# Complex-gate tree per head pair replaced by a real-decay tree over eight heads per chunk, with phases moved onto q and k

## Chip, cores and metric

One core of a Trainium2 chip runs the program. The metric is device time in microseconds (us) from the first to the last instruction of that core. Runs of the kernel before: 1729.12, 1729.69 and 1709.76 us, median 1729.12.

## What is computed

Four batches, eight heads, 768 tokens, head size 48; then a two-matrix block over 3072 tokens. Inputs are float32, the two weight matrices float64, the result float32.

```python
scale = np.minimum(mag, 0.999) / (mag + 1e-06)      # mag = |a_re + i a_im|
a = (a_re + 1j * a_im) * scale
for t in range(S):                                  # S is a 48 x 48 complex state per head
    S = a[:, :, t, :, None] * S + k[:, :, t, :, None] * v[:, :, t, None, :]
    y[:, :, t] = einsum('bhd,bhde->bhe', q[:, :, t], S.real)
x = y as (3072, 384)
h = x @ w_in                                        # 384 x 2048
out = (maximum(h, 0) + alpha * minimum(h, 0)) @ w_out   # 2048 x 384
```

## The kernel before, in words

A *unit* (`unit`, L182) is two heads of one batch over all 768 tokens: head 0 on partitions 0 to 47, head 1 on 64 to 111. There are 16 units, run two at a time. Each loads q, k, a_re, a_im and v (`load`, L87), makes the gates on VectorE (L193 to L209, with two RECIPROCALs), and climbs a binary tree of seven levels (h = 1, 2, ..., 64 tokens, L231 to L287). On a level TensorE multiplies k and q for all six 128-token chunks (L239, one matmul for the real part and one for the imaginary part, each with K = 48 rows and 128 weight columns), VectorE multiplies K, Q and T by complex products of the other half's gates (L256 to L279, four operations for each complex product, with two cross terms), and a predicated copy (L283) puts the level's products into the attention matrix A. Then the state passes from chunk to chunk (L289 to L314) and the result y comes from A times v and Q times the state (L317 to L331).

The second part (`mlp`, L335) takes one batch in two groups of 384 tokens: transposes of x (L343), 16 blocks of hidden features (three matmuls each, L352; two ScalarE activations L356 and L357; one VectorE operation L358), then three output blocks of 16 matmuls (L365), a copy (L368) and a store from GpSimd's queue (L370). The float64 weights are turned into float32 by `to_f32` (L111) in 40 pieces of one DMA, two ScalarE, four VectorE and two GpSimd operations each.

The order is written out by hand at L373 to L397: after every step of a unit one step of the second part of the *batch before* is issued (in the first batch a step of the weights). The second part of the last batch runs alone at the end. All loads go through SP's queue, in program order. Every float32 matmul appears as two records in the trace.

Of the kernel before, what the change touches and what calls it, by code (L numbers as in the profile page):

```python
# [9 lines left out]
U8 = mybir.dt.uint8  # L10
# [3 lines left out]
PSUM = bass.MemoryType.PSUM  # L14

# [3 lines left out]
SQ_FLOOR = 2.0 ** -116  # lower end of the square root's range  # L19
# A float64's high word, read as a float32: that of 2**-126, where float32's normal numbers begin.  # L20
# [4 lines left out]
def kernel(  # L25
    ctx: ExitStack,
    tc: tile.TileContext,
    q: bass.AP,      # (B, H/2, 2, D, S)
    k: bass.AP,      # (B, H/2, 2, D, S)
    v: bass.AP,      # (B, H/2, 128, S/128, 2*D)  # L30
    a_re: bass.AP,   # (B, H/2, 2, D, S)
    a_im: bass.AP,   # (B, H/2, 2, D, S)
    w_in: bass.AP,   # (H*D, DF)
    w_out: bass.AP,  # (DF, H*D)
    alpha: bass.AP,  # (128, DF/128)
    out: bass.AP,    # (B*S, H*D)
):
# [12 lines left out]

    A unit is two heads of one batch: head 0 on partitions 0.., head 1 on partitions 64.. .
    """
    nc = tc.nc
    B, HP, _, D, S = q.shape
    DM, DF = w_in.shape
    NCH = S // P            # chunks of a batch
    NK = DM // P
    NF = DF // P
    W = 64 + D              # partitions of a unit
    HC = P // 2             # tokens of a chunk that lie in second halves  # L60
    GC = NCH // 2           # chunks of one group of tokens in the second part
    GT = GC * P
    LEVELS = [1 << i for i in range(7)]

    consts = ctx.enter_context(tc.tile_pool(name="consts", bufs=1))
    ld = ctx.enter_context(tc.tile_pool(name="ld", bufs=1))
    work = ctx.enter_context(tc.tile_pool(name="work", bufs=2))
    ps2 = ctx.enter_context(tc.tile_pool(name="ps2", bufs=2, space=PSUM))
    ps1 = ctx.enter_context(tc.tile_pool(name="ps1", bufs=2, space=PSUM))

    def rows(i):
        return slice(64 * i, 64 * i + D)

# [1 line left out]
    q_buf = [ld.tile([W, S], F32, tag=f"q{i}", name=f"q{i}") for i in range(2)]  # L75
    a_buf = [ld.tile([W, 2, S], F32, tag=f"a{i}", name=f"a{i}") for i in range(2)]
    k_buf = [ld.tile([W, 2, S], F32, tag=f"k{i}", name=f"k{i}") for i in range(4)]
    for t in q_buf:
        nc.gpsimd.memset(t[32:64], 0.0)
    for t in a_buf:  # L80
        nc.vector.memset(t[32:64], 0.0)
    for t in k_buf:
        nc.gpsimd.memset(t[32:64, 0], 0.0)

    loaded = {}

    def load(u):  # L87
        b, hp = divmod(u, HP)
        qt, at, kt = q_buf[u % 2], a_buf[u % 2], k_buf[u % 4]
        vt = work.tile([P, NCH, 2 * D], F32, tag="v", name="v", bufs=4)  # L90
        for i in range(2):
            nc.sync.dma_start(at[rows(i), 0], a_re[b, hp, i])
            nc.sync.dma_start(at[rows(i), 1], a_im[b, hp, i])
        for i in range(2):
            nc.sync.dma_start(qt[rows(i)], q[b, hp, i])
            nc.sync.dma_start(kt[rows(i), 0], k[b, hp, i])
        nc.sync.dma_start(vt, v[b, hp])
        loaded[u] = (qt, at, kt, vt)

    load(0)  # L100
    load(1)
# [20 lines left out]
        # numbers below float32's normal ones become 0  # L122
# [4 lines left out]
        # sign, exponent and the first 20 bits of the mantissa  # L127
# [5 lines left out]
        # the other 32 bits, by the power of two  # L133
# [8 lines left out]
    def weights():  # L142
        if w_in.dtype == F32:
# [4 lines left out]
        for c in range(NK):  # L148
            for f in range(0, DF, 256):
# [8 lines left out]
    ident = consts.tile([P, P], F32, tag="ident")  # L158
    make_identity(nc, ident)
    masks = {}  # L160
    for h in LEVELS:
        nb = HC // h
        m = work.tile([P, nb, h], F32, tag="mask", name="mask")
        nc.gpsimd.memset(m, 1.0)
        nc.gpsimd.affine_select(out=m, in_=m, pattern=[[-2 * h, nb], [0, h]], base=0,
                                channel_multiplier=1, compare_op=ALU.is_ge, fill=0.0)
        nc.gpsimd.affine_select(out=m, in_=m, pattern=[[2 * h, nb], [0, h]], base=h - 1,
                                channel_multiplier=-1, compare_op=ALU.is_ge, fill=0.0)
        masks[h] = consts.tile([P, NCH, HC], U8, tag=f"mask{h}", name=f"mask{h}")
        nc.vector.tensor_copy(masks[h], m.rearrange("p n h -> p (n h)").unsqueeze(1)  # L170
                              .to_broadcast([P, NCH, HC]))

# [1 line left out]
    x_of = {}  # L174

    def halves(t, h):
        """A (re, im) or plain row of tokens as (..., block, half, token)."""
        if len(t.shape) == 3:
            return t.rearrange("p r (n s h) -> p r n s h", s=2, h=h)
        return t.rearrange("p (n s h) -> p n s h", s=2, h=h)  # L180

    def unit(u):  # L182
        b, hp = divmod(u, HP)
        qt, at, kt, vt = loaded.pop(u)
        Q = work.tile([W, 2, S], F32, tag="Q", name="Q")
# [13 lines left out]
        nc.scalar.activation(mag, sq, AF.Sqrt)  # L199
        # one Newton step brings the table's root to float32: twice the magnitude  # L200
        nc.vector.reciprocal(rec, mag)  # L201
        nc.vector.tensor_tensor(out=rec, in0=rec, in1=sq, op=ALU.mult)
        nc.vector.tensor_tensor(out=mag, in0=mag, in1=rec, op=ALU.add)
        nc.vector.tensor_scalar(out=rec, in0=mag, scalar1=0.5, scalar2=MAG_EPS, op0=ALU.mult, op1=ALU.add)
# [26 lines left out]
        for h in LEVELS:  # L231
# [16 lines left out]
            def over(t):  # L248
                return t.unsqueeze(2).to_broadcast(sh)
# [125 lines left out]
    for u in range(0, B * HP, 2):  # L375
        b = u // HP
        if u % HP == 0 and b:
            for _ in dense:
                pass
# [14 lines left out]
    for _ in dense:  # L394
        pass
# [40 lines left out]
```

## Time and profile before

| what | value |
|---|---|
| median of 3 runs | 1729.12 us |
| span of the profiled execution | 1729.1 us |
| mean granted TensorE clock | 0.834 of 2.4 GHz |
| TensorE busy | 1421.9 us |
| VectorE busy | 1326.3 us |
| ScalarE busy | 244.1 us |
| GpSimd busy | 169.0 us |
| moved by DMA | 42.28 MB, 18034 packets |

The span is the whole device time; nothing lies around it. "Busy" of TensorE counts any time with a matmul in flight, so it overstates useful work. DVE is VectorE, ACT ScalarE, POOL GpSimd, SP the queue of loads; PEld are TensorE's weight loads.

### The profile page before, as it was taken

Reading aid. Unit: us, or ns where it says so; the run is one execution under the profiler, and the core shown is the slowest. Engines: PE = TensorE matmul, PEld = TensorE weight load, DVE = VectorE, ACT = ScalarE, POOL = GpSimd, SP = SyncE. Lnnn points to the kernel's source line nnn. Section 1 sums busy time; section 2 is a strip of 40 time slices with the busy share of each in tenths; the row PEclk is TensorE's granted clock in tenths of the full one; section 3 lists DMA queues with packets and bytes.
Section 4 is the critical chain, followed back from the end, with each engine's and each line's share of the span. In section 5 each row is a group of like instructions: output and inputs, shape, how many; then the busy total and the mean of one; then the engine's idle time right before and its main releaser. Section 6 shows DMA issues by size and latency. Waiting matters only on the chain.

```text
span 1729.1 us, 21531 instructions
## 1 busy us (share of the span) xinstructions
PE 1421.9 (82%) x8808; PEld 1078.1 (62%) x8808; DVE 1326.3 (77%) x2298; ACT 244.1 (14%) x498; POOL 169.0 (10%) x153
## 2 busy tenths in 40 slices
PE   1456924558889998899889998899889998899998
PEld 1455824557656685678566775678566775678555
DVE  7999689995699829993799849982899749981210
ACT  2000111101201121001211120001201120001321
POOL 3222335551000000000000000000000000000000
PEclk9999999999979959775779868765779868665999
DMA  5211113100010001000010001000010000000000
GB/s 120 66 32 31 46 46 87 46 28 21 7 42 1 17 26 27 16 15 21 14 35 1 29 14 41 1 15 25 10 35 1 15 1 0 5 10 1 1 14 14
DMA packets 18034, 42.28 MB, mean 24 GB/s; under 512 B 3472, under 2 KB 3472, under 8 KB 17936
## 3 DMA queue, kind: packets, MB, share of 16 engines
q1 hardware_dynamic: 16400, 36.20, 8.0%
q0 software_dynamic: 1536, 4.72, 0.7%
q8 instruction: 69, 1.13, 0.3%
q14 instruction: 29, 0.24, 0.0%
HBM read 36.18 MB, written 4.72 MB: 24 GB/s over the span
## 4 chain that ended last, share of the span: by engine, by line
DVE 43%; issue 35%; PE 19%; ACT 1%; POOL 1%; DMA 0%; POOLq 0%; DVEq 0%; SPq 0%; ACTq 0%
PE ps_y L325 6%; DVE A L283 5%; PE ps_y L321 4%; DVE Q L268 4%; DVE rec L205 3%; DVE k L261 3%; DVE kx L260 3%; PE ps_o L365 3%; PE ps_lvl L239 2%; DVE rec L201 2%; DVE Q L270 2%; DVE tx L274 2%; PE ps_h L352 2%; DVE qx L267 2%; DVE Q L269 2%
## 5 line engine op out<-in xcount | busy, mean ns | idle before, releaser
L239 PE MATMUL ps_lvl<-Q,k 48*128 48x64 f32 x4992 | 426.3, 340 | 175.3 <-DVE A L283 160.2
L239 PEld LDWEIGHTS ps_lvl<-Q,k 48*128 48x128 f32 x4992 | 409.5, 249 | 231.4 <-issue 228.4
L352 PE MATMUL ps_h<-xT,w_in_sb 128*128 128x384 f32 x768 | 322.6, 576 | 0.0
L365 PE MATMUL ps_o<-w_out_sb,g 128*128 128x384 f32 x768 | 299.5, 535 | 21.7 <-DVE g L358 21.7
L352 PEld LDWEIGHTS ps_h<-xT,w_in_sb 128*128 128x128 f32 x768 | 168.9, 227 | 117.2 <-issue 44.1
L365 PEld LDWEIGHTS ps_o<-w_out_sb,g 128*128 128x128 f32 x768 | 153.9, 207 | 127.0 <-DVE g L358 24.7
L358 DVE SCALAR_TENSOR_TENSOR g<-neg,nal,g 128x384 f32<-128x384 f32 x128 | 81.1, 633 | 168.8 <-ACT neg L357 168.8
L325 PE MATMUL ps_y<-St,Q 48*128 48x48 f32 x640 | 167.2, 412 | 0.0
L283 DVE COPY_PREDICATED A<-mask,ps_lvl 128x384 f32<-128x384 uint8 x224 | 158.1, 720 | 0.0
L325 PEld LDWEIGHTS ps_y<-St,Q 48*128 48x128 f32 x640 | 141.5, 313 | 19.8 <-issue 5.8
L370 POOL DMA_DIRECT2D out_dram<-ot x24 | 13.1, 548 | 1237.6 <-ACT ot L368 1237.6
L218 PE MATMUL ps_diag<-q,k 48*128 48x128 f32 x384 | 55.7, 370 | 91.8 <-DVE A L221 83.3
L321 PE MATMUL ps_y<-v,A 128*128 128x48 f32 x384 | 115.7, 417 | 0.0
L356 ACT ACTIVATE g<-ps_h 128x384 f32<-128x384 f32 x128 | 62.9, 491 | 372.6 <-PE ps_h L352 367.0
L218 PEld LDWEIGHTS ps_diag<-q,k 48*128 48x128 f32 x384 | 47.7, 259 | 103.8 <-issue 58.8
L201 DVE RECIPROCAL rec<-mag 112x768 f32<-112x768 f32 x16 | 79.2, 4951 | 38.4 <-ACT mag L199 38.4
L261 DVE TENSOR_TENSOR k<-k,T 112x768 f32<-112x768 f32 x96 | 94.7, 987 | 11.8 <-PE ps_lvl L239 11.6
L321 PEld LDWEIGHTS ps_y<-v,A 128*128 128x128 f32 x384 | 91.5, 306 | 14.5
L267 DVE TENSOR_TENSOR qx<-Q,T 112x768 f32<-112x768 f32 x96 | 100.5, 1047 | 0.0
L139 POOL TENSOR_TENSOR rest<-rest,power 128x256 f32<-128x256 f32 (+1 forms) x40 | 74.3, 1857 | 233.6 <-DVE power L135 217.0
L268 DVE TENSOR_TENSOR Q<-Q,T 112x768 f32<-112x768 f32 x96 | 95.8, 998 | 0.0
L260 DVE TENSOR_TENSOR kx<-k,T 112x768 f32<-112x768 f32 x96 | 94.1, 981 | 0.0
(68 smaller groups left out, 1295.7 us busy)
## 6 DMA issues: line engine op xcount, KB each, us to landing
raw<-in_w_in_dram SPq DMA_DIRECT2D x24, 256.0 KB, 2.8
raw<-in_w_out_dram SPq DMA_DIRECT2D x16, 384.0 KB, 3.1
a<-in_a_re_dram SPq DMA_DIRECT2D x32, 144.0 KB, 3.3
a<-in_a_im_dram SPq DMA_DIRECT2D x32, 144.0 KB, 3.6
q<-in_q_dram SPq DMA_DIRECT2D x32, 144.0 KB, 2.8
k<-in_k_dram SPq DMA_DIRECT2D x32, 144.0 KB, 2.9
v<-in_v_dram SPq DMA_DIRECT2D x16, 288.0 KB, 2.8
out_dram<-ot POOLq DMA_DIRECT2D x24, 192.0 KB, 2.1
```

The lines of the kernel that those rows point to most:

```text
L201: nc.vector.reciprocal(rec, mag)
L218: nc.tensor.matmul(ps[:, i, c * P:(c + 1) * P], lhsT=kt[rows(i), 0, cols], rhs=qt[rows(i), cols], start=True, stop=True)
L239: nc.tensor.matmul(ps[:, i, c * HC:(c + 1) * HC], lhsT=kt[rows(i), r, cols], rhs=halves(Q[rows(i), r, cols], h)[:, :, 1], start=(r == 0), ...
L260: nc.vector.tensor_tensor(out=cross, in0=kf, in1=over2(second[:, 1]), op=ALU.mult)
L261: nc.vector.tensor_tensor(out=kf, in0=kf, in1=over2(second[:, 0]), op=ALU.mult)
L267: nc.vector.tensor_tensor(out=cross, in0=qs, in1=over2(first[:, 1]), op=ALU.mult)
L268: nc.vector.tensor_tensor(out=qs, in0=qs, in1=over2(first[:, 0]), op=ALU.mult)
L283: nc.vector.copy_predicated(halves(A[:, i].rearrange("p c t -> p (c t)"), h)[:, :, 1], masks[h].rearrange("p c (n h) -> p (c n) h", h=h), ...
L321: nc.tensor.matmul(y, lhsT=A[:, i, c], rhs=vt[:, c, i * D:(i + 1) * D], start=True, stop=(c == 0))
L325: nc.tensor.matmul(y, lhsT=Q[rows(i), r, c * P:(c + 1) * P], rhs=St[rows(i), c - 1, r], start=False, stop=(r == 1))
L352: nc.tensor.matmul(ps, lhsT=w_in_sb[:, kk, f * P:(f + 1) * P], rhs=xT[g][:, kk], start=(kk == 0), stop=(kk == NK - 1))
L365: nc.tensor.matmul(ps, lhsT=G[f][:, c * P:(c + 1) * P], rhs=w_out_sb[:, f], start=(f == 0), stop=(f == NF - 1))
```

## The change

The first part is rewritten.

- *Gates.* Now made for groups of 384 tokens (eight groups, `gates(g)`), with all 384 rows (8 heads x 48) on 128 partitions x 3. The magnitude goes to a DRAM scratch as a real decay. The unit phases are multiplied up over the tokens (a scan in blocks of 8, then 8 x 8, then 6, with a carry between the groups of a batch), and cos and sin go to the same DRAM scratch. Ten multiplications of a group are on VectorE for group 0 and on GpSimd for the others.
- *Unit.* Now one 128-token chunk of one batch with all eight heads (24 units). q and k are loaded twice, on partitions 0 to 47 and 48 to 95, and one VectorE operation multiplies them by cos and sin. After that one matmul with K = 96 stands for the real part, and decays are real: one VectorE operation per level for Q and K together; the products T of decays are made by GpSimd.
- *Array tiles.* A level's matmuls take 64 weight columns and 64 moving columns, for two heads in the two column halves. y is made transposed, from 64-row halves of v and the level's products, in 64 x 64 tiles; v's halves are loaded separately for each level (levels 2 to 32 through a DRAM copy, `first_halves`).
- *Second part.* y goes to DRAM and comes back as xT, with no transposes. The activation is one ScalarE and one VectorE operation (max(h,0) + alpha min(h,0) = h + (1 - alpha) max(-h,0)). The output store moves to SP.
- *Order.* Units start every 6 slots and take 11 steps, so two are alive; gates of the next group, v's copies and the second part of the group before are spread evenly over the slots (18 slots to a group).

The core of the diff (new lines; loads and most of the gates left out):

```python
def gates(g):
    mul = nc.vector if g == 0 else nc.gpsimd
    ab = work.tile([P, 2, NK, GT], F32, tag="ab", bufs=1)      # GT = 384 tokens, NK = 3
...
    nc.scalar.activation(d, c, AF.Abs_reciprocal_sqrt)
    nc.scalar.activation(e, d, AF.Square)
    mul.tensor_tensor(out=e, in0=e, in1=c, op=ALU.mult)
    nc.vector.scalar_tensor_tensor(out=d, in0=e, scalar=3.0, in1=d, op0=ALU.subtract, op1=ALU.mult)
    mul.tensor_tensor(out=c, in0=c, in1=d, op=ALU.mult)
    yield
...
    for j in range(1, L):                                      # L = 8, nb = 144
        nc.vector.tensor_tensor(out=mm, ...)                   # 4 * nb elements
        nc.vector.tensor_tensor(out=uv[:, 0, :, j], in0=mm[:, 0, 0], in1=mm[:, 1, 1], op=ALU.subtract)
        nc.vector.tensor_tensor(out=uv[:, 1, :, j], in0=mm[:, 0, 1], in1=mm[:, 1, 0], op=ALU.add)
...
def first_halves(b):                                           # 20 DMAs, DRAM to DRAM, runs of 96 elements
    for i, h in enumerate(LEVELS[1:-1]):
        for n in range(HP):
            nc.sync.dma_start(dst.rearrange("c (m h) e -> m h c e", h=h), src)
            yield
...
def load(u):                                                   # 16 DMAs on SP for one unit
    for i in range(2):
        rows = slice(i * D, (i + 1) * D)
        nc.sync.dma_start(KQ[rows, 0], qv[b, :, :, cols])      # rows of 128 tokens: 512 bytes
        nc.sync.dma_start(KQ[rows, 1], kv_in[b, :, :, cols])
    for i in range(2):
        rows = slice(i * D, (i + 1) * D)
        nc.sync.dma_start(PP[rows], scr[i, :, :, cg * P:(cg + 1) * P])
        nc.sync.dma_start(T[rows], scr[2, :, :, cg * P:(cg + 1) * P])
...
def unit(u, loaded):
    nc.vector.tensor_tensor(out=KQ, in0=KQ, in1=PP.unsqueeze(1).to_broadcast([D2, 2, H, P]), op=ALU.mult)
    yield
    def meet(name, weights, moving, n):
        t = ps.tile([P, HP, n], F32, tag="lv", bufs=2)
        for p in range(4):
            for i in range(2):
                nc.tensor.matmul(t[64 * i:64 * i + 64, p], lhsT=weights(4 * i + p),
                                 rhs=moving(KQ[:, 0, 4 * i + p]), start=True, stop=True)
        if name == HC:
            nc.scalar.copy(A[name], t)
        else:
            nc.vector.tensor_tensor(out=A[name], in0=t, in1=masks[name]..., op=ALU.mult)
...
    for h in LEVELS[1:]:                                       # Ts[2]: 512 elements, then 256, ... 8
        nc.gpsimd.tensor_tensor(out=Ts[2 * h], in0=t[:, :, 0], in1=t[:, :, 1], op=ALU.mult)
    yield
...
    for h in LEVELS[1:]:
        meet(h, first(h), second(h), HC)                       # first(h): a ScalarE copy into W
        nc.vector.tensor_tensor(out=both, in0=both, in1=Ts[h]..., op=ALU.mult)   # 1024 elements
        yield
...                                                            # 8 transposes, 8 matmuls: the state
    nc.gpsimd.tensor_tensor(out=St, in0=before, in1=Ts[P]..., op=ALU.mult)
    nc.vector.tensor_tensor(out=St, in0=St, in1=t, op=ALU.add)
    yield
    for s in range(2):
        for name in [1, "odd"] + LEVELS[1:]:
            for e in range(2):
                for i in range(2):
                    nc.tensor.matmul(o, lhsT=Vp[name][64 * i:64 * i + 64, s, e * D:(e + 1) * D],
                                     rhs=A[name][64 * i:64 * i + 64, 2 * s + e], ...)
...                                                            # 8 matmuls with the state before; y to DRAM
def mlp(g):
    nc.sync.dma_start(xT, ysc_of.pop(g).rearrange("(k p) s -> p k s", p=P))
    yield
...
    nc.scalar.activation(neg, t, AF.Relu, scale=-1.0)
    nc.vector.scalar_tensor_tensor(out=gt, in0=neg, scalar=rest_al[:, f:f + 1], in1=t,
                                   op0=ALU.mult, op1=ALU.add)
...
for _ in gates(0): pass
for _ in first_halves(0): pass
while live or slot <= NU * LAG + LAG or beside:                # LAG = 6, PER = 18 slots
    g, at = divmod(slot, PER)
    if at == 0 and g + 1 < NG:
        beside.append(spread(gates(g + 1), slot, slot + PER - LAG, 15))
    if at == LAG and 0 < g <= NG:
        beside.append(spread(mlp(g - 1), slot, slot + PER, 29))
    u, at = divmod(slot, LAG)
    if at == 0 and u < NU:
        live[u] = unit(u, loads.pop(u))
    for n in sorted(live): ...                                 # one step of each live unit
    if at == LAG - 1 and u + 1 < NU:
        loads[u + 1] = load(u + 1)
    ...                                                        # then the steps of beside that are due
```

## Rows read from the trace of the kernel before

**Rows 1.** The page's busy times, then its chain that ended last

```profile
PE 1421.9 (82%) x8808; PEld 1078.1 (62%) x8808; DVE 1326.3 (77%) x2298; ACT 244.1 (14%) x498; POOL 169.0 (10%) x153
...
DVE 43%; issue 35%; PE 19%; ACT 1%; POOL 1%; DMA 0%; POOLq 0%; DVEq 0%; SPq 0%; ACTq 0%
```

**Rows 2.** Windows: us, busy per engine (instructions), granted clock, DMA share, GB/s

```profile
129.70:172.90 43.20, 26.00 (x234) 25.21 (x234) 43.20 (x88) 3.20 (x9) 11.05 (x10) 1.00 0.10 31
...
475.50:518.70 43.20, 35.67 (x232) 25.49 (x232) 43.20 (x61) 4.31 (x9) 0.00 (x0) 0.74 0.18 42
907.80:951.00 43.20, 40.52 (x341) 29.45 (x340) 43.20 (x90) 5.78 (x12) 0.00 (x0) 0.92 0.01 1
1556.20:1599.40 43.20, 41.16 (x190) 35.14 (x189) 7.87 (x36) 4.69 (x12) 0.00 (x0) 0.50 0.00 0
1599.40:1729.10 129.70, 124.89 (x387) 73.21 (x386) 19.81 (x32) 31.66 (x72) 3.23 (x6) 0.99 0.02 10
```

**Rows 3.** TensorE's timeline: start us, length us, line, records, idle before

```profile
905.90 2.94 PE L239 MATMUL ps_lvl<-Q,k 48*128 48x64 f32 x48
...
1545.04 5.41 PE L239 MATMUL ps_lvl<-Q,k 48*128 48x64 f32 x48 [1.22 <-DVE A L283]
1552.76 2.37 PE L304 MATMUL ps_kv<-v,KT 128*64 128x48 f32 x40
1574.07 1.09 PE L321 MATMUL ps_y<-v,A 128*128 128x48 f32 x4
1575.09 1.09 PE L325 MATMUL ps_y<-St,Q 48*128 48x48 f32 x4
...
1600.93 30.48 PE L352 MATMUL ps_h<-xT,w_in_sb 128*128 128x384 f32 x94
```

**Rows 4.** VectorE's groups by line and shape: busy us, mean ns of one

```profile
L358 DVE SCALAR_TENSOR_TENSOR g<-neg,nal,g 128x384 f32<-128x384 f32 x128 | 81.1, 633 | 168.8 <-ACT neg L357 168.8
L201 DVE RECIPROCAL rec<-mag 112x768 f32<-112x768 f32 x16 | 79.2, 4951 | 38.4 <-ACT mag L199 38.4
L270 DVE TENSOR_TENSOR Q<-Q,qx 112x384 f32<-112x384 f32 x112 | 65.7, 587 | 0.0
L208 DVE TENSOR_TENSOR a<-a,rec 112x1536 f32<-112x1536 f32 x16 | 28.6, 1786 | 0.0
L203 DVE TENSOR_TENSOR mag<-mag,rec 112x768 f32<-112x768 f32 x16 | 15.3, 954 | 0.0
L125 DVE SCALAR_TENSOR_TENSOR top<-top,raw 128x256 f32<-128x256 f32 x24 | 10.5, 438 | 12.0 <-ACT top L124 12.0
L129 DVE TENSOR_SCALAR num<-top 128x256 uint32<-128x256 uint32 x24 | 6.8, 284 | 0.0
L279 DVE TENSOR_TENSOR T<-T,tx 112x12 f32<-112x12 f32 x16 | 3.2, 199 | 0.0
```

**Rows 5.** GpSimd beside VectorE: timeline, start us, length us

```profile
189.83 0.72 POOL L139 TENSOR_TENSOR rest<-rest,power 128x256 f32<-128x256 f32 x1 [2.58 <-DVE power L135]
...
254.43 0.99 POOL L139 TENSOR_TENSOR rest<-rest,power 128x384 f32<-128x384 f32 x1 [3.30 <-DVE power L135]
...
341.74 8.24 POOL L140 TENSOR_TENSOR w_out_sb<-num,rest 128x384 f32<-128x384 f32 x1
...
349.04 1.03 DVE L283 COPY_PREDICATED A<-mask,ps_lvl 128x384 f32<-128x384 uint8 x2
...
355.11 1.75 DVE L268 TENSOR_TENSOR Q<-Q,T 112x768 f32<-112x768 f32 x1
```

**Rows 6.** ScalarE's groups by line and shape

```profile
L193 ACT ACTIVATE Q<-a 112x1536 f32<-112x1536 f32 x16 | 23.9, 1494 | 2.7 <-DMA a<-in_a_im_dram 2.7
L193 ACT ACT_TABLE_LOAD x1 | 1.3, 1283 | 6.4 <-DMA a<-in_a_im_dram 6.4
```

**Rows 7.** DMA: the load queue's packets; a load; one issue on SP

```profile
q1 hardware_dynamic: 16400, 36.20, 8.0%
...
k<-in_k_dram SPq DMA_DIRECT2D x32, 144.0 KB, 2.9
...
4.77 0.42 SPq L96 DMA_DIRECT2D k<-in_k_dram  x1
```

More of the change, by code (lines that the diff above doesn't have):

```diff
@@ L71, in rows @@
[L71 to L90, printed above, removed]
-        for i in range(2):
[L92 to L98, printed above, removed]
@@ L100, with halves, mask @@
-    load(0)
-    load(1)
+    dram = ctx.enter_context(tc.tile_pool(name="dram", bufs=2, space=DRAM))
+    ps = ctx.enter_context(tc.tile_pool(name="ps", bufs=1, space=PSUM))
+    def halves(t, h):
+        return t.rearrange("p (n s h) -> p n s h", s=2, h=h)
+    ident = consts.tile([P, P], F32, tag="ident")
+    make_identity(nc, ident)
+    masks = {}
+    def mask(name, h, s):
+        m = work.tile([P, P // h, h * s], F32, tag="mask", name="mask", bufs=1)
+        nc.gpsimd.memset(m, 1.0)
+        nc.gpsimd.affine_select(out=m, in_=m, pattern=[[-h, P // h], [0, h * s]], base=0,
+                                channel_multiplier=1, compare_op=ALU.is_ge, fill=0.0)
+        nc.gpsimd.affine_select(out=m, in_=m, pattern=[[h, P // h], [0, h * s]], base=h - 1,
+                                channel_multiplier=-1, compare_op=ALU.is_ge, fill=0.0)
+        masks[name] = consts.tile([P, HC * s], F32, tag=f"mask{name}", name=f"mask{name}")
+        flat = m.rearrange("p n h -> p (n h)")
+        for i in range(2):
+            nc.gpsimd.tensor_copy(masks[name][64 * i:64 * i + 64],
+                                  flat[64 * i:64 * i + 64, HC * s * i:HC * s * (i + 1)])
@@ L142, in weights @@
     def weights():
+        al = work.tile([P, NF], F32, tag="al", name="al", bufs=1)
+        nc.sync.dma_start(al, alpha)
+        nc.vector.tensor_scalar(out=rest_al, in0=al, scalar1=-1.0, scalar2=1.0, op0=ALU.mult, op1=ALU.add)
         if w_in.dtype == F32:
@@ L147, in weights @@
         src = w_in.bitcast(U32).rearrange("(c p) (f two) -> p c f two", p=P, two=2)
-        for c in range(NK):
-            for f in range(0, DF, 256):
+        for f in range(0, DF, 256):
+            for c in range(NK):
                 to_f32(w_in_sb[:, c, f:f + 256], src[:, c, f:f + 256])
@@ L155, in weights @@
             yield
[L158 to L171, printed above, removed]
@@ L374 @@
-    dense = weights()
[L375 to L379, printed above, removed]
-            dense = mlp(b - 1)
-            next(dense)
-        live = [unit(u), unit(u + 1)]
-        step = 0
-        while live:
-            for g in list(live):
-                if next(g, live) is live:
-                    live.remove(g)
-                next(dense, None)
-            step += 1
-            if step == 3:
-                for w in (u + 2, u + 3):
-                    if w < B * HP:
-                        load(w)
@@ L394 @@
-    for _ in dense:
+    state = {}
+    ysc_of = {}
+    vsc_of = {}
+    def first_halves(b):
+        vsc_of[b] = dram.tile([len(LEVELS) - 2, NCH, 2, HC, 2 * D2], F32, tag="vsc", name="vsc")
+        for i, h in enumerate(LEVELS[1:-1]):
+            for n in range(HP):
+                src = v[b, n].rearrange("(m s h) c e -> s m h c e", s=2, h=h)[0]
+                dst = vsc_of[b][i, :, n // 2, :, (n % 2) * D2:(n % 2 + 1) * D2]
+                nc.sync.dma_start(dst.rearrange("c (m h) e -> m h c e", h=h), src)
+                yield
@@ L395, with spread @@
+    def spread(w, start, end, n):
+        return [start + (end - start) * i / n for i in range(n)], w
+    for _ in gates(0):
         pass
-    for _ in mlp(B - 1):
+    for _ in first_halves(0):
         pass
+    for name in ["odd"] + LEVELS[:-1]:
+        mask(name, 1 if name == "odd" else name, 2 if name == 1 else 1)
+    STEPS = 11
+    LAG = 6
+    NU = B * NCH
+    PER = GC * LAG
+    beside = [spread(weights(), 0, PER, 41)]
+    live = {}
+    loads = {0: load(0)}
+    slot = 0
+    while live or slot <= NU * LAG + LAG or beside:
+        g, at = divmod(slot, PER)
+        if at == 0 and g + 1 < NG:
+            beside.append(spread(gates(g + 1), slot, slot + PER - LAG, 15))
+        if at == 0 and g % 2 == 0 and g + 2 < NG:
+            beside.append(spread(first_halves(g // 2 + 1), slot, slot + PER, 21))
+        if at == LAG and 0 < g <= NG:
[3 more added lines that the diff above has]
+            live[u] = unit(u, loads.pop(u))
+        for n in sorted(live):
+            if next(live[n], live) is live:
+                del live[n]
+        if at == LAG - 1 and u + 1 < NU:
+            loads[u + 1] = load(u + 1)
+        for due, w in list(beside):
+            while due and due[0] < slot + 1:
+                due.pop(0)
+                next(w, None)
+            if not due:
+                for _ in w:
+                    pass
+                beside.remove((due, w))
+        slot += 1
```

439 lines of the change are left out of this document (258 added, 181 removed).

## The prediction

> **What bounds the kernel now.** First the busy times and the chain [rows 1]: TensorE 1421.9 and VectorE 1326.3 of 1729.1 us, so neither fills the span; the chain gives VectorE 43%, TensorE 19%, waits of a queue ("issue") 35%. The two take turns. Then the windows [rows 2]. In a batch's tree (907.8 to 951.0) VectorE is busy without a gap and TensorE 40.5 of 43.2. In a batch's end (1556.2 to 1599.4) VectorE has 7.9, TensorE 41.2 at a granted clock of 0.50: the y matmuls. Behind the last batch (1599.4 to 1729.1) the second part runs alone at 0.99. So the tree is VectorE's, the y stage TensorE's, and 129.7 us lie outside both. The span is the whole time and equals the median, 1729.12.
>
> **Part 1, second part on TensorE: unchanged.** 94 records of 384 columns took 30.48 us, 0.324 each [rows 3]. There are 1536, 498 us, or 62 for each of eight groups; the two groups at the end took 129.7, 65 each [rows 2]. It remains a floor, but only one group (65) now runs alone at the end, not two.
>
> **Part 2, TensorE of the first part.** A new unit has 64 level matmuls, 64 for y, 8 with the state before, 8 for the state (two records each) and 8 transposes (one each): 296 records, 888 to a group of three units. The number hardly falls: 24 x 296 less what the first and last chunks of a batch lack is 6,944, against 8808 - 1536 = 7,272 before. What changes is the price of one. Full-array y matmuls took 1.02 us for four, start to start: 0.255 each at clock 0.50. Level matmuls with 128 weight columns took 5.41/48 = 0.113 at 0.50 and 2.94/48 = 0.061 in a faster stretch. The state matmuls, 64 weight columns in two column halves, took 2.37/40 = 0.059 at 0.50 [rows 3]. New levels and y have that last shape, so I take 0.059: 52 us a group. Upper bound 0.113 (100 a group), lower 0.030, half of 0.059, if the same shape follows the clock from 1.2 to 2.4 GHz (27 a group).
>
> Switching between full array, halves and quarters is added: some 50 times a group. Four L321 and four L325 records stand 1.02 us apart though their row shapes differ [rows 3], the same 0.255 as in a row, so I can't find over 0.04 us a switch: 2 us a group. The Trainium skill ("TensorEngine Tiling (Array Packing)", Key Properties) says that changing the tiling mode, not just the tile, drains the engine. The trace shows no drain of a size that matters; by the full length of a y record for each switch the sum would be 13 us a group and not 2.
>
> Waits in a group: xT's landing 2.9 [rows 7], since the first matmuls are issued right behind its load, and about 5 for the round trips over one PSUM buffer in the state step. With the switches, 10. The second part at a clock of 0.85 (the mean before was 0.834, the tree had 0.92) is 62/0.85 = 73. **TensorE's group: 73 + 52 + 10 = 135 us.**
>
> **Part 3, VectorE.** A tensor operation costs 0.587 for 384 elements, 0.954 for 768, 1.786 for 1536 and 0.199 for 12 [rows 4]: about 0.19 + 1.04 ns an element. The two reciprocals (L201 79, L205 as long) and the cross terms go. A new unit has one operation of 2048 elements (2.3), seven of 1024 (8.8), three of 512 (2.2), six masks of 256 (2.8) and one of 384 (0.6): 16.7 us, 24 units 400. Gates of a group: six of 1152 (1.39 each, 8.3), seven steps of the scan with 576 + 144 + 144 (10.3), some 39 of under 80 elements (8), the rest 4: 31; eight groups and ten more of 1152 in the first: 262. The activation stays at 81 [rows 4]. The weights' conversions, two operations like L125 and two like L129 each [rows 4], are 1.44 in 24 pieces and by size 1.9 in 16: 65. Sum 808 against 1326. **A group: 50 + 31 + 10 = 91.**
>
> **Part 4, GpSimd and the port.** An operation of 256 elements took 0.72 and of 384 0.99 [rows 5]: 0.18 + 2.1 ns an element. A unit adds 1016 elements in seven (3.4) and 384 (1.0): 13 a group; gates add ten of 1152 (2.6 each): 26. Together 39 a group, and 66 for the weights in the first. But the two engines hinder each other: behind unbroken VectorE work the same 384 elements took 8.24 and ended when VectorE came to an operation that reads PSUM, and a VectorE operation of 0.95 took 1.75 beside it [rows 5]. If nothing overlaps, VectorE and GpSimd need 91 + 39 = 130 a group; if everything does, 91. Both lie under TensorE's 135, so I cost this at nothing in a full group; without that cover it is rival B.
>
> **Part 5, ScalarE.** 1.49 for 1536 elements [rows 6], about 1 ns an element: W copies, KT, y and gates come to some 45 us a group. Hidden.
>
> **Part 6, DMA.** All pieces of q, k, decays and phases are 512 bytes, v's 384. A unit has 3072 + 512 + 768 + 640 packets and 384 of y, 5,376; with gates, v's copies, xT, out and weights about 186,000, against 16,400 for 36.2 MB [rows 7], and some 123 MB. Packets of 2 KB took 106 ns (10% of 16 engines over 43.2 us for 31 GB/s, 654 packets), those of 3 KB 211 (18%, 42 GB/s, 590 packets) [rows 2]. Small ones aren't shown. By bytes 512 B would take 26 ns (38 us a group), as many packets at 211 would take 306 a group. I take 53, half of the nearest row: 77 us a group, hidden under 135. SP issues some 75 DMAs a group at 0.42 [rows 7], 31 us. Its one order matters: the load of unit u+1 stands behind the y store of unit u-1. From there: 1 us of copies, the store, 8 issues (3.3) beside 3072 packets (10), 2.9 to land: 15 us, while some 13 us (under two slots of 7.5) lie before its first use. I cost 2 us a unit, within the 10 above.
>
> **The sum.**
> - Start: gates(0) has nothing beside it. 16 VectorE operations of 1152 (22), its small ones 23, ScalarE in between 9 and four table loads of 1.28 [rows 6] 5, load and store 6. Then 20 copies of v stand ahead of load(0) (8 us of issues, 7680 packets, 25), and load(0) 5 behind it: 95 us.
> - Group 0 has no second part, but the weights: VectorE 50 + 31 + 65 = 146, GpSimd 39 + 66 = 105. Bounds 146 and 251 by the port; I take 200, the middle, since both shapes stand in rows 5.
> - Group 1 has the second part in 12 of its 18 slots: 135 - 24 = 111.
> - Groups 2 to 7: 6 x 135 = 810.
> - The last unit's end and the last third of the second part before: 30. The last group alone: 65.
> 95 + 200 + 111 + 810 + 30 + 65 = **1311, say 1310 us**; 1200 to 1430 as its own range (a group at 121 to 150).
>
> **Rivals.**
> - *A, better packed (1080).* Records follow the clock, 0.030 at 2.4 GHz: 62 + 27 + 10 = 99 for TensorE, VectorE with part of GpSimd near 110, then the bound. 85 + 160 + 86 + 6 x 110 + 25 + 65 = 1081. For it: 0.061 against 0.113 in one shape [rows 3]. Against: in stretches of short matmuls the clock was 0.50 [rows 2].
> - *B, the port and waits in order (1570).* VectorE and GpSimd exclude each other (130), each group's gates make three trips ScalarE, GpSimd, VectorE (two of 1.2, a table load and 2.6: 6 us each, 18) and the loads come 5 us late three times (15): 163 a group. 100 + 250 + 139 + 6 x 163 + 35 + 65 = 1567. For it: 8.24 for 0.99 [rows 5]. The Trainium skill ("SBUF — State Buffer", SBUF: two separate sides) calls the shared port pair an exclusive lock that a VectorE operation with two SBUF inputs holds too against a GpSimd operation that reads SBUF; by that rule 130 and not 91 is the price, and the rows agree. Against: masks, activations and waits leave gaps.
> - *C, small packets (slower).* The loads become the bound: 186,000 packets at over 139 ns on 16 engines fill 1,620 us, which with about 110 before and behind is the time before; that is the point from which it decides. At the 211 of the 3 KB packets: 2450 + 110 = 2560. Against: 2 KB took only 106. The Trainium skill ("DMA: Bandwidth & Descriptors", Specifications) wants 512 bytes for line rate and gives read-modify-write below it, where v's pieces lie; no run here shows a packet of data under 512 bytes other than alpha's.
> - *D, the tiles don't overlap (1660).* The change doesn't do what it says: 0.113 a record, 73 + 100 + 10 = 183 a group: 100 + 200 + 159 + 6 x 183 + 35 + 65 = 1657. Against: L304 [rows 3].
>
> **Chances.** Forecast 0.50, A 0.20, B 0.20, D 0.05, C 0.05. Faster by over 2% (about what a measurement tells from no change) are the first four but for a sliver of D: 0.93; same 0.02; slower 0.05. The range takes in most of A and B: 1110 to 1580, leaving out A's lower half, B's upper end, D and C.
>
> **What would show it.** Right: groups of some 135 us; TensorE busy nearly throughout at 0.8 to 0.9; level and y records near 0.06 start to start; VectorE about 810 us busy or a little more for the port; GpSimd operations of 1152 from 2.6 to 8; DMA share near a half. Wrong: TensorE waiting on VectorE's gate operations or on KQ's loads (B), packets over 100 ns (C), records over 0.1 (D), a clock near 1.0 with records of 0.03 (A).

## The result, and the profile after

The changed kernel takes 1433.48 us, median of four runs (1428.88 to 1436.41), against 1724.15 for the kernel before (four runs, 1709.76 to 1729.69): a ratio of 0.833, 95% interval 0.8288 to 0.8371. The direction was as forecast and the time lies in the range given, 1110 to 1580. It is 123 us above the forecast of 1310 and 3 us above the upper end of the forecast's own range, 1430.

The page of the changed kernel first: busy times, TensorE's tenths and clock in 40 slices, the load queue, the chain. They answer to [rows 1, 7].

```profile
PE 917.7 (64%) x8480; PEld 604.8 (42%) x8480; DVE 861.9 (60%) x1357; ACT 331.2 (23%) x606; POOL 452.9 (32%) x375
...
PE   0011050505156699996568776996387879999998
...
PEclk9999999999999899898579995995599899999999
...
q1 hardware_dynamic: 195952, 123.52, 33.3%
...
PE 41%; DVE 31%; DMA 8%; POOL 5%; ACT 5%; issue 4%; SPq 4%; DVEq 0%; ACTq 0%; POOLq 0%
```

TensorE fell from 1421.9 to 917.7 and VectorE from 1326.3 to 861.9, both more than the time did. Now TensorE has work in 918 us of a span of 1430.8 and none in 513. So the question is where those 513 us lie. Windows from group start to group start (a group is three units, and starts with the first VectorE operation of its first unit, L360) tell it; columns as in [rows 2]:

```profile
0.00:96.00 96.00, 0.00 (x0) 0.00 (x0) 43.84 (x94) 14.03 (x13) 27.88 (x41) 1.00 0.32 81
96.00:320.00 224.00, 55.99 (x744) 44.19 (x744) 136.66 (x238) 46.42 (x95) 90.56 (x86) 1.00 0.36 97
320.00:461.00 141.00, 65.55 (x840) 52.06 (x840) 119.86 (x176) 37.70 (x68) 84.57 (x62) 1.00 0.41 114
461.00:676.00 215.00, 182.81 (x1280) 113.76 (x1280) 107.89 (x175) 48.31 (x89) 46.30 (x32) 0.90 0.31 76
676.00:784.00 108.00, 71.58 (x702) 48.54 (x702) 86.43 (x138) 31.32 (x54) 50.18 (x35) 0.72 0.46 116
784.00:981.00 197.00, 157.56 (x1421) 102.17 (x1420) 108.99 (x160) 42.63 (x77) 45.73 (x32) 0.85 0.32 79
981.00:1093.00 112.00, 70.86 (x695) 48.31 (x696) 88.72 (x139) 32.78 (x55) 52.52 (x40) 0.73 0.49 123
1093.00:1203.00 110.00, 92.08 (x933) 58.29 (x931) 86.87 (x132) 31.40 (x56) 39.67 (x26) 0.91 0.37 98
1203.00:1364.00 161.00, 159.00 (x1681) 101.60 (x1681) 72.83 (x96) 36.93 (x81) 15.53 (x24) 0.99 0.23 59
1364.00:1430.80 66.80, 62.28 (x192) 35.92 (x190) 9.83 (x16) 9.67 (x20) 0.00 (x0) 1.00 0.03 12
```

TensorE is idle for 96 us before the first unit, 168 in group 0, 75 in group 1 and some 173 behind. Groups 0, 2 and 4 last 224, 215 and 197; 3, 5 and 6 last 108 to 112. Groups 0, 2 and 4 are those in which a batch's copies of v (`first_halves`, L321) are issued. By idle time, though, only the start and groups 0 and 1 stand out: groups 2 and 4 have 32 and 39 us without TensorE work, no more than groups 3 and 5 (36 and 41). They last longer because more of the second part runs in them: 384 and 296 of its 1536 matmul records, against 88 in each of groups 3 and 5.

What TensorE waited for longest, before a unit's first matmuls, is the product that needs the unit's loads (229.7 us, 98 of it at the start):

```profile
L369 PE MATMUL ps_lv<-KQ 96*64 96x64 f32 (+1 forms) x1152 | 75.7, 295 | 251.9 <-DVE KQ L360 229.7
```

The second part starts late. A line's summary of instructions (ns min/median/max, then first and last start in us):

```profile
L482 PE MATMUL ps_h<-xT,w_in_sb x768: 486/486/1009, 487.3 to 1394.3; 128*128 128x384 f32 x192
```

The first matmul of the second part comes at 487, in group 2. Two of its groups fall into group 2 (TensorE 183 of 215 us busy). The groups of costs (columns as in [rows 4]), two of TensorE, two of VectorE, one of GpSimd:

```profile
L482 PE MATMUL ps_h<-xT,w_in_sb 128*128 128x384 f32 x768 | 285.0, 521 | 7.2 <-DVE g L488 5.0
L495 PE MATMUL ps_o<-w_out_sb,g 128*128 128x384 f32 x768 | 268.6, 505 | 3.5 <-ACT ot L500 3.4
...
L413 DVE TENSOR_TENSOR KQ<-KQ,T 96x1024 f32<-96x1024 f32 x144 | 218.7, 1519 | 9.7 <-PE ps_lv L369 9.6
...
L171 DVE TENSOR_TENSOR tmp<-ab 128x576 f32<-128x576 f32 x56 | 68.0, 1214 | 1.1
...
L138 POOL TENSOR_TENSOR tmp<-tmp 128x1152 f32<-128x1152 f32 x7 | 22.9, 3267 | 7.2 <-DVE tmp L137 7.2
```

The second part takes 285.0 + 268.6 = 553.6, 69 a group; all other TensorE work is the remaining 364, 45.5 a group.

And SP's queue, from its timeline (start us, length us; an issue that stands late has waited in the queue's order). Between unit 0's load, which ends at 97.15, and unit 1's:

```profile
97.77 0.43 SPq L263 DMA_DIRECT2D raw<-in_w_in_dram  x1
...
107.54 0.34 SPq L263 DMA_DIRECT2D raw<-in_w_in_dram  x1
107.92 1.25 SPq L321 DMA_DIRECT2D vsc<-in_v_dram  x2
118.96 0.35 SPq L263 DMA_DIRECT2D raw<-in_w_in_dram  x1
...
134.83 0.33 SPq L263 DMA_DIRECT2D raw<-in_w_in_dram  x1
...
149.40 0.33 SPq L263 DMA_DIRECT2D raw<-in_w_in_dram  x1
149.78 0.43 SPq L334 DMA_DIRECT2D KQ<-in_q_dram  x1
...
179.79 0.59 SPq L350 DMA_DIRECT2D VL<-vsc  x1
```

Each load of a piece of the weights (L263) waits until the one raw buffer is free, 4 to 14 us. Unit 1's load stands behind five of them and is broken by three more, so unit 1 starts at 179, 83 us behind unit 0. Later, in group 2, stores do the same. Output stores (L502), which the change put on this queue, wait for the second part's results and are issued at 541.01, 552.38 and 563.79, with copies between them. Then a store of y (L469) waits 26.2 us, and the load of unit 8 is first issued behind it, at 596.69:

```profile
594.97 0.99 SPq L469 DMA_DIRECT2D ysc<-yT  x2
```

SP's three longest waits over the whole span (total, times, longest) are two kinds of stores and the weight loads:

```profile
SPq L469 <- ACT yT L468: 229.4, 26, 62.6
SPq L502 <- ACT ot L500: 204.6, 17, 40.9
SPq L263 <- DVE top L273: 180.5, 36, 22.3
```

### The profile page after: what moved, and what is told of

The parts are those of the page before. It is cut to its first block, busy times and chain, and to the rows that moved or that the text cites. A ratio compares the mean times of both kernels' runs of the same rounds, so it can differ in the third digit from the quotient of the medians.

```text
span 1430.8 us, 21018 instructions
## 1 busy us (share of the span) xinstructions
PE 917.7 (64%) x8480; PEld 604.8 (42%) x8480; DVE 861.9 (60%) x1357; ACT 331.2 (23%) x606; POOL 452.9 (32%) x375
## 2 busy tenths in 40 slices
DMA packets 196050, 124.87 MB, mean 87 GB/s; under 512 B 71024, under 2 KB 190832, under 8 KB 195952
## 3 DMA queue, kind: packets, MB, share of 16 engines
q1 hardware_dynamic: 195952, 123.52, 33.3%
## 4 chain that ended last, share of the span: by engine, by line
PE 41%; DVE 31%; DMA 8%; POOL 5%; ACT 5%; issue 4%; SPq 4%; DVEq 0%; ACTq 0%; POOLq 0%
PE ps_o L495 14%; PE ps_h L482 13%; PE ps_lv L369 6%; DVE KQ L413 6%; DVE tmp L171 4%; PE ps_y L453 3%; DMA raw<-in_w_in_dram 3%; PE ps_kv L430 2%; DVE KQ L360 2%; SPq L321 2%; DVE ab L175 2%; DVE top L273 2%; DVE ab L155 2%; PE ps_kt L426 1%; DVE ab L174 1%
## 5 line engine op out<-in xcount | busy, mean ns | idle before, releaser
L482 PE MATMUL ps_h<-xT,w_in_sb 128*128 128x384 f32 x768 | 285.0, 521 | 7.2 <-DVE g L488 5.0
L495 PE MATMUL ps_o<-w_out_sb,g 128*128 128x384 f32 x768 | 268.6, 505 | 3.5 <-ACT ot L500 3.4
L369 PE MATMUL ps_lv<-KQ 96*64 96x64 f32 (+1 forms) x1152 | 75.7, 295 | 251.9 <-DVE KQ L360 229.7
L413 DVE TENSOR_TENSOR KQ<-KQ,T 96x1024 f32<-96x1024 f32 x144 | 218.7, 1519 | 9.7 <-PE ps_lv L369 9.6
L369 PE MATMUL ps_lv<-KQ,W 96*64 96x64 f32 x1920 | 107.4, 270 | 150.8 <-ACT W L382 150.7
L369 PEld LDWEIGHTS ps_lv<-KQ,W 96*64 96x64 f32 x1920 | 88.7, 176 | 188.6 <-ACT W L382 176.7
L375 DVE TENSOR_TENSOR A<-ps_lv,mask 128x512 f32<-128x512 f32 (+1 forms) x144 | 66.9, 464 | 154.8 <-PE ps_lv L369 154.3
L488 DVE SCALAR_TENSOR_TENSOR g<-neg,rest_al,ps_h 128x384 f32<-128x384 f32 x128 | 77.8, 609 | 118.5 <-ACT neg L486 118.4
L382 ACT COPY W<-KQ 96x512 f32<-96x512 f32 x120 | 74.9, 624 | 285.2 <-DVE KQ L413 205.2
L401 POOL TENSOR_TENSOR T<-T 96x256 f32<-96x256 f32 (+1 forms) x144 | 91.5, 635 | 84.0 <-DVE KQ L413 64.3
L453 PE MATMUL ps_y<-A,VL 64*48 64x64 f32 x1920 | 68.2, 260 | 69.4 <-DVE A L375 69.3
L395 POOL TENSOR_TENSOR T<-T 96x512 f32<-96x512 f32 x24 | 32.8, 1369 | 225.9 <-DMA T<-scr 195.2
L360 DVE TENSOR_TENSOR KQ<-KQ,PP 96x2048 f32<-96x2048 f32 x24 | 61.7, 2570 | 43.6 <-DMA V<-in_v_dram 39.5
L171 DVE TENSOR_TENSOR tmp<-ab 128x576 f32<-128x576 f32 x56 | 68.0, 1214 | 1.1
```

Of the source, the lines that this page charges most:

```text
L171: nc.vector.tensor_tensor(out=mm, in0=uv[:, :, :, j].unsqueeze(2).to_broadcast([P, 2, 2, nb]), in1=uv[:, :, :, j - 1].unsqueeze(1).to_broa ...
L360: nc.vector.tensor_tensor(out=KQ, in0=KQ, in1=PP.unsqueeze(1).to_broadcast([D2, 2, H, P]), op=ALU.mult)
L369: nc.tensor.matmul(t[64 * i:64 * i + 64, p], lhsT=weights(4 * i + p), rhs=moving(KQ[:, 0, 4 * i + p]), start=True, stop=True)
L375: nc.vector.tensor_tensor(out=A[name], in0=t, in1=masks[name].unsqueeze(1).to_broadcast([P, HP, n]), op=ALU.mult)
L382: nc.scalar.copy(W.rearrange("p n t -> p (n t)").rearrange("p (m h) -> p m h", h=h), halves(KQ[:, 1].rearrange("p n t -> p (n t)"), h)[:, ...
L401: nc.gpsimd.tensor_tensor(out=Ts[2 * h], in0=t[:, :, 0], in1=t[:, :, 1], op=ALU.mult)
```

## The experiments

Theories after this profile: (1) the copies of v in SP's order make groups 0, 2 and 4 long; (2) the chain of the weights' conversions keeps the second part from starting; (3) GpSimd's wide operations stretch VectorE's through the shared port (rival B's mechanism). The rival to each is that its idle time is filled from elsewhere.

| run | time us | TensorE busy, idle | first of second part at |
|---|---|---|---|
| changed kernel | 1433.5 | 917.7, 513 | 487 |
| e1 no copies later | 1332.4 | 898.1, 432 | 563 |
| e2 two raw, two KQ buffers | 1413.8 | 912.4, 500 | 379 |
| e3 copies on ScalarE's queue | 1444.3 | 885.3, 557 | 745 |
| e5 no conversions | 1294.5 | 901.3, 391 | 280 |
| e6 copies all at the start | 1346.6 | 898.8, 446 | 582 |
| e7 copies split | 1399.5 | 917.6, 480 | 451 |
| e4 gates on VectorE | 1343.1 | 900.6, 441 | 460 |
| e9 e6 + eight y buffers | 1347.7 | 899.0, 447 | 580 |
| e10 e6 + e4 | 1251.5 | 886.2, 364 | 524 |
| e11 e10 + e2 | 1182.2 | 861.0, 320 | 320 |
| e12 e10 + T on VectorE | 1239.7 | 881.9, 356 | 517 |
| e13 e11 + T on VectorE | 1165.8 | 854.0, 313 | 324 |

Idle is the span less TensorE's busy time. All but the first and the last row are single runs; the changed kernel's four lie within 0.5%, so that differences under some 10 us say little.

**e1: copies left out.**

```diff
-            beside.append(spread(first_halves(g // 2 + 1), slot, slot + PER, 21))
+            vsc_of[g // 2 + 1] = vsc_of[0]
```

> Leaves out the copies of v's halves for batches 1 to 3 (60 of 80 DRAM-to-DRAM transfers); those batches read batch 0's copies, so their y differs. Theory 1 (the copies stand on SP's queue ahead of the units' loads): the groups that carry copies (0, 2, 4: 224, 215 and 197 us from first unit to first unit) shrink, 2 and 4 to the 110 of their neighbours, and the time falls from 1433 by 150 to 250 us. Rival (the port of VectorE and GpSimd, or the gates, make these groups long): groups 2 and 4 stay near 200 and the time falls by under 40.

Measured 1332.4, 101 less: more than the rival's 40, less than the 150 to 250 of theory 1. SP's waits from unit 0's start to 320, of the changed kernel and then of this one (total, times, longest):

```profile
SPq L263 <- DVE top L273: 135.8, 27, 22.3
```

```profile
SPq L263 <- DVE top L273: 54.3, 14, 6.8
```

In the same stretch weight loads waited half as often for VectorE (22 were issued in it, against 28), and groups 0 and 1 last 126 each instead of 224 and 141. The weights come later for it (second part at 563). Groups 2 and 4 last 140 and 92, but group 3 lasts 308: no unit starts between 568 and 796, while the second part catches up; from there TensorE is nearly full.

**e2 and e5: the conversions.**

```diff
-        raw = work.tile([P, DM, 2], U32, tag="xT", name="raw", bufs=1)[:, 0:n]
+        raw = work.tile([P, DM, 2], U32, tag="raw", name="raw", bufs=2)[:, 0:n]
-        KQ = work.tile([D2, 2, H, P], F32, tag="KQ", name="KQ", bufs=3)
+        KQ = work.tile([D2, 2, H, P], F32, tag="KQ", name="KQ", bufs=2)
```

> Two buffers for a raw piece of the weights instead of one (room for them comes from KQ, two buffers instead of three). Theory 2 (the 40 conversions are one chain over one buffer, load, ScalarE, VectorE, release, some 9.5 us a piece, and this chain sets the time until the second part starts at 487 us): the start of the second part falls to 330 to 420 and the time by 70 to 150 us. Rival (the first groups are bound by VectorE, GpSimd and their port): under 30 us.

In e5 the pieces of both matrices are not loaded or converted; two constants stand in their place.

> Leaves out the conversion of the weights (both matrices are set to a constant), with its loads, ScalarE, VectorE and GpSimd work. Theory 2: the second part starts near 300 instead of 487 us and the time falls by 120 to 190 us. Rival (copies and gates set the first two groups): the time falls by under 60 us.

With two buffers the second part starts 108 us earlier, as theory 2 has it, but the end comes only 20 earlier, as the rival has it; group 0 still lasts 228. Without conversions the start is 208 earlier and the end 139, as theory 2 has it. Group 0 then lasts 131 though it has the same copies, but groups 2 and 4 still 200. So in group 0 it is the two together, copies that place unit loads behind weight loads that wait.

**e3, e7 and e6: what of the copies costs.**

```diff
-                nc.sync.dma_start(dst.rearrange("c (m h) e -> m h c e", h=h), src)
+                nc.scalar.dma_start(dst.rearrange("c (m h) e -> m h c e", h=h), src)
```

> The same 80 copies of v's halves, issued on ScalarE's queue instead of SP's. Theory 1 with SP's order as the cause: most of what leaving out the copies gains, 100 to 200 us. Rival within it (the copies fill few DMA engines, whatever queue issues them): under 50 us, and the loads of a unit still land late.

Measured 1444.3, 11 more. The first unit starts at 69, 27 earlier, but the issues now stand in front of ScalarE's work. ScalarE's timeline of this kernel, its queue (ACTq) and the first operation behind:

```profile
68.62 28.33 ACTq L321 DMA_DIRECT2D vsc<-in_v_dram  x9
97.00 0.43 ACT L272 ACTIVATE top<-raw 128x256 f32<-128x256 f32 x1 [47.10 <-issue]
```

The conversions ran late and the second part started at 745. The gain that theory 1 expected did not come: another queue alone doesn't help.

> The copies stay where they are, but those of 16 and 32 rows are cut into one DMA for each outer index, so that each spreads over the DMA engines. Theory 1 (few engines to a copy make the issue of one last up to 4 us, and SP's queue behind it late): issues fall under 1 us each, groups 2 and 4 to 120 to 160, the time to 1280 to 1370. Theory 2 (their number and place in SP's order matter, not how many engines carry them): groups 2 and 4 stay near 200 and the time at 1400 to 1460.

The edit cuts each copy of 16 or 32 rows into one DMA for each outer index (`dst[m], src[m]`). Measured 1399.5, 34 less: between the two theories. 10 of it is the start (first unit at 86). Group 0 still lasts 212, groups 2 and 4 206 and 200. The length of an issue is the smaller part.

```diff
-    for _ in gates(0):
-        pass
-    for _ in first_halves(0):
-        pass
+    g0 = gates(0)
+    next(g0)
+    for b in range(B):
+        for _ in first_halves(b):
+            pass
+    for _ in g0:
+        pass
...
-        if at == 0 and g % 2 == 0 and g + 2 < NG:
-            beside.append(spread(first_halves(g // 2 + 1), slot, slot + PER, 21))
```

> The copies of v for all four batches are issued at the start, behind the first store of gates(0), each piece with the outer dimensions unrolled so that its rows spread over 16 DMA engines; nothing else moves and all work is done. Theory (it is the copies' place beside the units that makes groups 2 and 4 last about 200 us): both groups fall to 110 to 150, the first unit starts later, at 100 to 140 instead of 96, and the time is near that of the kernel without the later copies plus the later start: 1330 to 1380. Rival (groups 2 and 4 are long because the second part falls into them in dense runs, copies or not): they stay at 170 to 220 and the time at 1420 to 1470.

e6 (with e7's cut, and a scratch for each batch) does all the copies and takes 1346.6, 14 above e1, while its first unit starts 18 later. So neither the copies' traffic nor their number costs the time. Place and cut together are worth 87; against e7, which has the same cut, the place alone is worth 53. SP's timeline of e6: unit 1's load begins right behind one weight load and is broken by three more, so that four stand ahead of its end and not eight.

```profile
117.26 0.48 SPq L339 DMA_DIRECT2D KQ<-in_q_dram  x1
...
158.14 0.49 SPq L355 DMA_DIRECT2D VL<-vsc  x1
```

Groups 0 to 2 of e6 last 126, 126 and 141, and group 4 lasts 91, but group 3 lasts 308, as in e1. In SP's timeline no piece of a unit's load is issued between 617.17 and 780.71; what lies there are loads and stores of the gates, loads of xT and output stores. Whether that order holds the units up there was not tested by itself. With e4 on top (e10) group 3 lasts 236, with the second raw buffer too (e11) 119.

**e4: GpSimd and the port.**

```diff
-        mul = nc.vector if g == 0 else nc.gpsimd
+        mul = nc.vector
```

> The ten wide products and sums of a group's gates go to VectorE in every group, as in the first one; GpSimd loses about 190 us of work, VectorE gains ten operations of 1.3 us in seven groups, 91 us. Theory (the port and the trips between engines cost little beside TensorE and the waits): 1410 to 1460. Rival B of the prediction (the two engines shut each other out, so that GpSimd's operations of 2.2 to 3.3 us hold VectorE): VectorE's other operations get shorter (the 1024-element ones from 1.52 to 1.25) and the time falls to 1330 to 1400.

Measured 1343.1, 90 less: rival B's expectation. The edit takes away GpSimd's work beside VectorE and also the gates' trips between the two engines; which share of the 90 is whose was not tested. Busy times and the 1024-element group of this kernel:

```profile
PE 900.6 (67%) x8480; PEld 592.5 (44%) x8480; DVE 852.3 (64%) x1427; ACT 328.7 (25%) x606; POOL 286.2 (21%) x305
```

```profile
L413 DVE TENSOR_TENSOR KQ<-KQ,T 96x1024 f32<-96x1024 f32 x144 | 182.8, 1269 | 7.5 <-PE ps_lv L369 7.3 <-issue 0.2
```

VectorE has 70 operations of 1.35 to 1.52 us more, 98 us, and is busy 10 us *less*: some 108 us of its time in the changed kernel was stretch beside 167 us of GpSimd work. The 1024-element operation fell from 1.519 to 1.269, the 1.25 that the prediction took. This agrees with the rule of the Trainium skill that rival B cited ("SBUF — State Buffer", SBUF: two separate sides).

**e9: do units wait for y's buffer?** `bufs=NG` on `ysc`, on top of e6.

> As the kernel with all copies at the start, and y's DRAM buffer has one copy for each of the eight groups instead of two, so that no unit has to wait for the second part of two groups before. Theory (units stand still while the second part waits for the weights): the gaps between units go, the second parts run without a break from about 480 on, and the time falls to 1200 to 1320, 60 to 120 below the kernel with the copies at the start. Rival (the second part is limited by TensorE's queue order and by the weights alone): within 25 of that kernel.

1347.7 against 1346.6: no. The theory fell, and group 3 still lasts 308.

**e10 to e13: do the gains add?**

> Both edits that gained most by themselves: all copies of v at the start, and the gates' ten wide products and sums on VectorE in every group. If the two causes are apart (copies beside the units; GpSimd stretching VectorE), their gains add: 1346.6 less about 90 is 1240 to 1275. If both only took the same idle time of TensorE, 1300 to 1340.

> The kernel with both edits, and two raw buffers for the weights' conversions instead of one (and two KQ buffers instead of three, for the room). Theory (the conversions' chain over one buffer sets the start of the second parts): the first of them starts about 100 earlier, and now that the copies are gone from the middle the end follows by half of it or more: 40 to 100 below the kernel with one buffer. Rival (the end is set by the units' own path and TensorE, the early second parts only wait later): within 25 of it.

> The kernel with both edits, and the units' products of phases' decays (T2 and T4 to T128, seven operations a unit, 124 us of GpSimd in the changed kernel) also on VectorE, which gains about 24 operations of 0.7 and 144 of 0.2 to 0.4, some 60 us. If GpSimd's work costs VectorE about 0.6 us of stretch for each us, as the gates' did, the stretch that goes, some 70, pays for it: within 25 of the kernel with both edits. If these short operations hide in VectorE's waits and stretch nothing, 30 to 70 slower.

> All the edits that gained: copies of v at the start, gates' wide products and units' T products on VectorE, two raw buffers with two of KQ. It does all the work of the reference. If T's products pay as they did with one raw buffer (12 less), 1160 to 1180. If VectorE, busy 871 of 1180 us without them and nearly throughout up to 740, is by now the bound beside TensorE, the added operations cost their own net 18 us or more: 1190 to 1230.

e12 and e13 put the two T products (`nc.gpsimd.tensor_tensor` at L395 and L401) on `nc.vector`. The copies at the start, with their cut, are worth 87 alone and 92 on top of e4; the gates' engine 90 alone and 95 on top of e6: they add. The second raw buffer is worth 20 in the changed kernel and 69 once the two are in (the second part then starts 204 earlier, where about 100 was expected). Whether the copies, the gates or both had held its gain up was not tested. T's products gave 12 and 16, little beside the spread of single runs, but not the loss that was one of the expectations.

e13 does all the work and beats both kernels: 1165.8, median of four (1162.8 to 1168.7), ratio to the kernel before 0.6787, interval 0.6754 to 0.6821. Its busy times, and four windows from group start to group start (groups 0, 1, 2 and 5):

```profile
PE 854.0 (73%) x8480; PEld 549.4 (47%) x8480; DVE 886.8 (76%) x1595; ACT 328.5 (28%) x606; POOL 187.5 (16%) x137
```

```profile
114.00:263.00 149.00, 53.09 (x720) 41.91 (x720) 140.79 (x268) 50.90 (x99) 85.87 (x52) 1.00 0.51 143
263.00:416.00 153.00, 100.11 (x986) 65.92 (x987) 148.60 (x252) 52.99 (x96) 58.93 (x32) 0.82 0.40 113
416.00:523.00 107.00, 99.81 (x1029) 63.06 (x1027) 97.62 (x178) 35.86 (x64) 2.98 (x2) 0.94 0.43 114
...
748.00:862.00 114.00, 104.58 (x1080) 66.58 (x1072) 103.12 (x190) 36.38 (x66) 1.66 (x2) 0.96 0.40 116
```

No group lasts 200 us any more. Groups 0 and 1 are still the longest, and VectorE is nearly full in them (141 of 149, 149 of 153). In groups 2 and 5 TensorE and VectorE are both busy for about nine tenths, and TensorE is without work for 7 and 9 us.

## Why the prediction was right, and where it was not

The forecast was 1000 us of TensorE work (8 x (73 + 52)) and 311 without any; measured were 918 and 513. Two errors of opposite sign: 82 too much work, 202 too little waiting. That the time lies in the range is in part luck, and in part the range's width. The prediction's own signs say the same: TensorE was busy for 64% and not nearly throughout, groups lasted 108 to 224 and not some 135, and one sign of rival B came, TensorE waiting on KQ's loads.

- **Start, 95 us.** The first unit starts at 96, by errors that cancel. The gates' last store was out at 58, not 65; from the first issue of load(0) to the first unit took 13, not 5. The copies took 24.5 (58.03 to 82.57) where the step had 25, but it had them as packets beside 8 us of issues, and here it was the issues that lasted.
- **TensorE's group: 73 + 52 + 10 = 135.** The second part is 69, the first 45.5 a group: 114 of work where I had 125. A record came to 0.051 over all (45.5 over 888), with 0.059 taken; rival D (0.113) fell. But the reading by the clock behind these prices does not hold: 48 level records took 5.41 in the kernel before at a granted clock of 0.50 (at 1545.04, [rows 3]), and the same 5.41 at 341.89, in a stretch at 1.00 throughout. So what set these prices is open, and that 0.059 came near is in part luck. The timeline and the windows before:

```profile
341.89 5.41 PE L239 MATMUL ps_lvl<-Q,k 48*128 48x64 f32 x48 [2.92 <-DVE A L283]
...
43.20:430.00 386.80, 223.86 (x1717) 208.91 (x1717) 347.25 (x636) 42.56 (x94) 135.94 (x80) 1.00 0.16 44
```

Dense stretches even ran as rival A has it. In the changed kernel's timeline at 1203.16, beside the second part and at a granted clock of 1.00, 16 level records began 0.52 us before the next 16, 0.033 each.

```profile
1203.16 0.69 PE L369 MATMUL ps_lv<-KQ,W 96*64 96x64 f32 x16
1203.68 0.66 PE L369 MATMUL ps_lv<-KQ 96*64 96x64 f32 x16
```

- **Waits, 10 a group.** This term failed. Groups 3 and 5 have 36 and 41 us without TensorE work. The number counted xT, PSUM and switches, and the loads at 2 us a unit. In group 3 (676 to 784) TensorE waited 15.5 us for ScalarE's copies W, 13.5 for VectorE's products A and 6.0 for a unit's loads; group 5 is alike. In e13 groups 2 and 5 are down to 7 and 9, so 10 was right only once copies, gates, T's products and the raw buffer were changed.
- **Group 0, "I take 200", and group 1 with the second part in 12 of 18 slots.** Measured 224 and 141. The size lay in its bounds (146 to 251), but by another cause than the port (with the gates on VectorE, e4, group 0 lasts 210; without the later copies, e1, 126), and the weights were not ready at its end: I priced 40 conversions by what the engines do (VectorE 65, GpSimd 66) and not by their chain over one raw buffer, 40 pieces from the first load at 97.8 to the last product at 481.6, 9.6 us each. The second part began at 487 and not near 330 (95, 200 and a third of 111). e5 prices the conversions at 139 of the total.
- **Copies of v in groups 0, 2 and 4.** The prediction has SP's order as what matters, for a load behind a y store, but puts 2 us a unit on it, and prices the copies as 25 us at the start and packets later. Place and issue of the copies cost 87 (e6), the place 53 of it. That unit loads then stand behind weight loads is shown for group 0; for later groups, behind stores of y and of outputs, it is read from timelines alone (SP waited 229.4 us for y in 26 of 48 stores), and how much of that cost time is open. Stores on another queue were not tried.
- **Part 4, the port, "I cost this at nothing in a full group".** It cost 90 with the gates' trips (e4). The reason I gave against B (masks, activations and waits leave gaps) did not hold; its 163 a group was never reached, since groups without copies lasted 108 to 112.
- **Part 3, VectorE 808.** Measured 861.9, some 108 of it stretch beside the gates' GpSimd work: so VectorE's own work came to some 754, less than the 808.
- **Part 6, packets, 53 ns.** 33.3% of 16 engines over 1430.8 us for 195,952 packets is 39 ns each. In the trace the 61,440 packets of 384 bytes took 25.6 ns on average and the 82,944 of 512 bytes 36.5, so nothing shows a price on pieces under 512 bytes. Rival C, which needs 139, is out.

## To carry to other kernels

When the busiest engine's work is cut by a third, price the waits anew. For each queue that takes its instructions in order, list what stands ahead of the next unit's load and what each of those waits for; a cheap DMA can move a load behind an expensive wait, and so can a store. Price a chain through one buffer by its round trip, not by the engines' work in it. And GpSimd is not free beside a busy VectorE: moving ten wide operations *onto* the busier engine made it less busy.

## What the runs showed of the hardware that was not expected

The copies' issue time depends on their shape. Those with 2 or 4 outer rows hold the queue: of the twelve ahead of unit 0's load the first five were issued in 0.7 to 1.0 us each, the last seven in 1.9 to 4.0. Cut by the outer index, 24 took 15.75 us, 0.66 each. SP's timeline of the changed kernel and then of e7:

```profile
58.03 24.54 SPq L321 DMA_DIRECT2D vsc<-in_v_dram  x12
```

```profile
61.12 15.75 SPq L326 DMA_DIRECT2D vsc<-in_v_dram  x24
```

The granted clock did not tell how long the short matmuls lasted, as in the kernel before (5.41 us at 1.00 and at 0.50). Windows from 440 to 470 of e6 and then of e9, and 16 level records in each:

```profile
440.00:470.00 30.00, 16.46 (x222) 13.18 (x218) 28.77 (x76) 9.37 (x21) 16.69 (x14) 1.00 0.42 113
...
457.25 1.12 PE L374 MATMUL ps_lv<-KQ,W 96*64 96x64 f32 x16 [0.30 <-ACT W L387]
```

```profile
440.00:470.00 30.00, 16.35 (x224) 13.26 (x224) 29.40 (x77) 8.35 (x19) 18.41 (x15) 0.50 0.47 121
...
455.28 1.12 PE L374 MATMUL ps_lv<-KQ,W 96*64 96x64 f32 x16 [0.30 <-ACT W L387]
```

At 2.4 GHz granted in the one and 1.2 in the other, with TensorE busy for about 16 of 30 us in both, 16 records took the same 1.12 us; beside the second part, where TensorE had no gap, they took 0.69. The mean granted clocks of the two runs, 0.973 and 0.901, left no mark on their times, 1346.6 and 1347.7.
